# Reordering the start of a fused mLSTM and squared-ReLU FFN kernel: earlier weight words, later transposes and scores

## The chip, the cores and the metric

The kernel runs on one core of a Trainium2 chip. The time is that of one execution on the device, in microseconds. The kernel before has a median of 488.39 us in three runs (487.24 to 491.11). A profile is one further execution, recorded by the hardware profiler.

Engines are named as in the profile: PE is the matrix engine (PEld its weight loads), DVE the vector engine, ACT the scalar engine, POOL the GpSimd engine, SP the engine that issues most of the DMAs.

## The reference

There are four batches, eight heads, 768 steps and a head width of 40. For each step, an mLSTM cell updates a matrix state C and a vector n with stabilised gates, and reads them out with q:

```python
for t in range(S):
    m_new = np.maximum(f_gate[:, :, t] + m, i_gate[:, :, t])
    f_stab = np.exp(f_gate[:, :, t] + m - m_new)
    i_stab = np.exp(i_gate[:, :, t] - m_new)
    C = f_stab * C + i_stab * einsum('bhd,bhe->bhde', vt, kt)
    n = f_stab * n + i_stab * kt
    y[:, :, t] = sigmoid(o_gate[:, :, t]) * (C q) / max(|n . q|, 1)
```

The result is laid out as x with 3072 tokens of width 320. The FFN is `h = max(x @ w_in, 0)` and `out = (h * h) @ w_out`, with w_in of 320 x 2048 and w_out of 2048 x 320. The two weights come as 64-bit floats and are handed to the kernel as pairs of 32-bit words.

## The kernel before

The sequence is cut into 24 chunks of 128 steps, numbered from 0, six to a batch; chunk `s` has all eight heads. Two chunks make one of twelve groups of 256 tokens, on which the FFN works. The kernel is written in one order by hand: each engine runs its instructions in the order in which the program issues them, and waits where its operands or buffers are not ready.

For a chunk, `load_part(s, i)` loads k, q or v (i = 0, 1, 2) and `load_A(s)` loads A, the running sums of the log decay, spread over all partitions; `load_o(s)` loads the o gate. All these are DMAs on SP's queue. A is computed once for all chunks by `do_gates` on DVE, written to DRAM by `store_A`, and can be loaded from there only after that. Chunks 0 and 1 don't load A but build it on PE (`spread_mask`, `spread_A`). Then, for each chunk:

- `transposes(s)`: PE turns k and q (L553), and ACT, or DVE for chunk 1, copies them out of PSUM (L556).
- `scores(s)`: PE multiplies k and q (L587).
- `mask` (POOL, L472) and `weigh(s)` (ACT, L515 and L519) make the decay weights W; `values` (POOL, L536) scales v by W's last column for the state.
- `weighted(s)`: DVE multiplies the scores with W (L601).
- `attend(s)`: PE forms the read-out of the old state (L637), the state's increment dC (L649) and the read-out within the chunk (hp, L660). DVE adds them (L668, L831) and renews the state (L676, L678).
- `normalise(s)` makes x on DVE (L833 to L840), and `turn_rows(s)` turns x on PE (L870, L872), with a copy to xT on ACT (L875).

FFN1 of a group is done in four parts of four blocks of w_in (`ffn1(g, pp)`: L896 and L907), each followed on ACT by a relu (L920) and a square (L926). The three scratch banks `ps_at` in PSUM are used in turn by the transposes, scores, x turns and the first read-out, so a turn can wait for the copy of an older one.

The weights are brought into 32-bit floats while the attention runs, in 18 pieces: ten of w_in, numbered 0 to 9, then eight of w_out. The class `Rounding` does each piece in three steps. `fetch` loads its raw words (SP, L206). `words` splits them in two on ACT (L216, L218). `join` puts them together with three operations on DVE (L227, L231, L232) and an addition on POOL (L236), and then issues the fetch of a further piece. There are three buffers for raw words and some space lent by another tile, so a fetch waits for the join that reads its buffer. FFN1's part 0 needs pieces 0, 1 and 2, part 1 needs 3 and 4, part 2 needs 5, 6 and 7, and part 3 needs 8 and 9.

After a written-out start for chunks 0 to 2, a loop over `u` from 0 to 7 does chunks 2 to 5 in half steps, each with one FFN1 part. A second loop over `n` does the rest: parts of FFN1 and FFN2 in turn, four to a chunk, with the attention of a chunk laced in (`attend_begin`, `attend_end`). In this stretch FFN2 uses a fast product with seven multiplications for eight, which needs sums of blocks of w_out: `sums_of_weights(i)` on DVE, of which number 3 is L961, in place on w_out. `attend_begin` ends with a one-element operation on DVE (L718), for which the second half of the chunk's products on PE (L757 in `attend_end`) waits. `spread_slots(b)` issues three DMAs on POOL (L383, L385) that copy batch b's rows of A into another order in DRAM. `sums_of_x` (POOL, L1048 and L1051) makes the sums of xT for the fast FFN1.

Of the kernel before, what the change touches and what calls it, by code (L numbers as in the profile page):

```python
# [29 lines left out]
def kernel(  # L30
# [148 lines left out]
    class Rounding:  # L179
# [11 lines left out]
        def fetch(self):  # L191
            n = len(self.raws)
            if n == len(pieces):
                return
            dst, srcs = pieces[n]
            if n < LENT and n % NRAW == NRAW - 1:
                at = 2 * NPAIR * P
                raw = lent_t[:, at : at + 2 * WIDE].bitcast(I32).rearrange("p (c w) -> p c w", w=2)
            else:
                raw = conv.tile([P, WIDE, 2], I32, name="raw", bufs=NRAW - 1)  # L200
            self.raws.append(raw)
            for rows, src in srcs:
                to = raw[rows, : dst.shape[1]]
                if len(src.shape) == 4:
                    to = to.rearrange("p (a f) w -> p a f w", a=src.shape[1])
                nc.sync.dma_start(to, src)  # L206
# [200 lines left out]
    def load_o(s):  # L407
        b, c = divmod(s, NB)
        r, (s0, s1) = next((r, (a, z)) for r, (a, z) in enumerate(RUNS) if a <= s < z)
        if s == s0:  # L410
            st["og", r] = ld.tile([P, 4, H, D], F32, name="og")
        og = st.setdefault(s, {})["og"] = st["og", r][:, s - s0]
        nc.sync.dma_start(og, o_gate[b, :, c * P : (c + 1) * P, :].rearrange("h p d -> p h d"))
# [7 lines left out]
    def load_A(s):  # L421
        b, c = divmod(s, NB)
        d = st.setdefault(s, {})
        A = ld.tile([P, H, P], F32, name="A_bc", bufs=2)
        d["A"] = [A]
        if s >= ROT:
            d["A"] = [A[:].rearrange("p (x own) t -> p x (own t)", own=2)]
            for m in range(2):
                nc.sync.dma_start(
                    A[HALVES[m]].rearrange("p h t -> p (h t)"),  # L430
                    A_slots[b, c, m].rearrange("x own t -> (x own t)").unsqueeze(0).to_broadcast([DP, H * P]),
                )
            return
        nc.sync.dma_start(
            A[:].rearrange("p h t -> p (h t)"),
            A_d[c, b * H : (b + 1) * H].rearrange("h t -> (h t)").unsqueeze(0).to_broadcast([P, H * P]),
        )

    def spread_mask(s):
        H2 = H // 2  # L440
        A = ps_h.tile([P, H2, P], F32, name="A_ps", tag="h_ps")
        nc.tensor.matmul(
            A[:], lhsT=ident_h[:], rhs=later_h[:].unsqueeze(1).to_broadcast([P, H2, P]), start=True, stop=True,
            skip_group_check=True,
        )
        st.setdefault(s, {}).setdefault("A", []).append(A)
# [100 lines left out]
    def transposes(s, o=(False, False)):  # L547
        d = st[s]
        kqT(s)
        for i, n in enumerate(("kT", "qT")):  # L550
            tp = bank(o[i])
            for j in range(PR):
                nc.tensor.transpose(  # L553
                    tp[:, j, :], d["kq"][:, i, 2 * j : 2 * j + 2, :].rearrange("p h d -> p (h d)"), ident[:],
                )
            (nc.vector.tensor_copy if s == 1 else nc.scalar.copy)(d[n], tp)  # L556
# [355 lines left out]
    def ffn1(g, pp):  # L912
        ffn1_main(g, pp)
        ffn1_rest(g, pp, st["half"][0])
# [220 lines left out]
    def idle(n):  # L1135
        t = ps_h.tile([P, W], F32, name="idle", tag="h_ps")
        for _ in range(n):
            nc.tensor.matmul(
                t[:], lhsT=zeros[:, :1].to_broadcast([P, P]), rhs=zeros[:, :1].to_broadcast([P, W]), start=True, stop=True,
            )  # L1140
# [5 lines left out]
    def load_part(s, i):  # L1146
        b, c = divmod(s, NB)
        dst, src = load_parts(s)[i]
        nc.sync.dma_start(dst, src[b, :, c * P : (c + 1) * P, :].rearrange("h p d -> p h d"))
# [10 lines left out]
    load_part(1, 2)  # L1160
    load_o(0)
    load_o(1)
    idle(12)
    transposes(0)
    idle(4)
# [3 lines left out]
    rounding.words()  # L1169
    store_A()  # L1170
    load_A(2)
    load_part(2, 0)
    load_part(2, 1)
    fetch(1)
    load_part(2, 2)
    fetch(1)
    spread_A(0)
    turn_gates(i_sb, b_T)
    rounding.join()
    load_A(3)  # L1180
    load_part(3, 0)
    load_part(3, 1)
    eA_turned = turn_gates(A_sb, eA_T, later=True)
    weigh(0)
    eA_turned()
    transposes(1, (False, True))
    spread_mask(1)
    spread_mask(1)
    spread_A(1)
    scores(0)  # L1190
    weigh(1)
    scores(1, (True, True))
    rounding.words()
    first.close()
    ffn = ctx.enter_context(tc.tile_pool(name="ffn", bufs=2))
    before = ExitStack()
# [5 lines left out]
    half_tanh(0)  # L1202
    half_tanh(1)
    weighted(0)
    weighted(1)
    attend(0)
    rounding.join()
    load_part(3, 2)
    load_o(2)
    load_o(3)  # L1210
    rounding.words()
    normalise(0)
    attend(1)
    rounding.join()
    turn_rows(0)
    transposes(2)
    idle(2)
    turn_rows(1)
    rounding.words()
    scores(2)  # L1220
    weigh(2, masked=True)
    decay_old(2)
    rounding.join()


# [2 lines left out]
    for u in range(8):  # L1228
        s = 2 + u // 2
        relu_half()  # L1230
        if u % 2 == 0:
            if u == 0:
                ffn1(0, 0)
            else:
                if u == 2:
                    idle(3)
                if s - 1 < X_SQ:
                    turn_rows(s - 1)
                if u == 4:
                    square_half()  # L1240
                scores(s)
                ffn1(u // 4, u % 4)
            if u == 2:
                rounding.words()
                weigh(4, masked=True, vw=False)
                decays(4)
                rounding.words()
            weighted(s)
            if u == 0:
                mask(s + 1)  # L1250
                rounding.step()
            if u == 2:
                rounding.join()
                rounding.join()
                mask_W(4)
                values(4)
                rounding.words()
            else:
                if u == 0:
                    relu_half()  # L1260
                weigh(s + 1, masked=(u != 6), vw=(u == 6))
                if u == 4:
                    mask_W(5)
                square_half()
                if u > 0:
                    scale_q(s)
        else:
            if u == 1:
                half_tanh(2)
                half_tanh(3)  # L1270
            if u < 7:
                load_A(s + 2)
            for r in {1: (), 3: (5, 6), 5: (7,), 7: ()}[u]:
                load(r)
            if u == 5:
                for r in range(4, 8):
                    half_tanh(r)
            if s < X_SQ:
                attend(s)
            else:  # L1280
                attend_begin(s)
                attend_end(s)
                store_num(s)
            if u == 3:
                square_half()
            if u != 3:
                rounding.join(fetch=u < 7)
            if u == 1:
                load(4)
                values(s + 1)  # L1290
            if s < X_SQ:
                normalise(s)
            if u == 3:
                rounding.join()
            if u == 5:
                pair_up(7)
            if u == 7:
                load_A(7)
            if u > 4:
                load_num(s)  # L1300
            transposes(s + 1, (True, True))
            rounding.words()
            ffn1(u // 4, u % 4)
            if u != 3:
                square_half()
            if u == 5:
                decays(5)
            if u == 7:
                normalise_turned(4)
                store_rows(4)  # L1310
                rounding.fetch()
                rounding.join()
        if u < 4:
            load_o(4 + u)
        while rounding.done < NEXT[u]:
            if u == 1 and rounding.done + 1 == NEXT[u]:
                rounding.join()
            else:
                rounding.step()
        if u == 6:  # L1320
            load_squares(7)
        for x in WIN_SUMS.get(u, ()):
            sums_of_win(x)
# [21 lines left out]
    for n, (which, g, i) in enumerate(parts):  # L1345
# [52 lines left out]
        if n == 8:  # L1398
            sums(1, slice(0, NPAIR), (3,))
        if n == 9:  # L1400
            sums_of_weights(3)
            sums(1, slice(0, NPAIR), (4,))
            sums_of_weights(2)
            turn_squares(6)
# [65 lines left out]
            do(load, s + 4)  # L1470
        if n == 4:
            sums_of_weights(1)
        if n == 3:
            turn_halves()
        if n in (9, 25):
            spread_slots(2 + n // 25)
        if at == 0:
            ffn1_square()
# [33 lines left out]
```

## Time and profile before

| | |
|---|---|
| median of three runs | 488.39 us (487.24 to 491.11) |
| profiled execution | 489.48 us, with a span of 487.7 us from the first to the last instruction |
| mean granted PE clock | 0.997 of full speed |
| PE busy | 478.5 us (98% of the span) |
| DVE, ACT, POOL busy | 340.6 us, 243.1 us, 227.4 us |
| DMA | 69.92 MB, mean 143 GB/s |

By stages, DMA is near or above a full share of its sixteen engines from 10 to 70 us (0.93 to 1.17 in each 10 us) and at 0.75 to 0.78 from 140 to 300 us. ACT is busy for 9.96 of the 10 us from 40 to 50 and for 9.87 from 60 to 70.

The profile gives, for each engine, busy time and the idle time ahead of an instruction with the event that ended it. The chain of work that ended last is followed back from the last instruction, at each step to what released it. A busy PE does not say at what clock it ran; that stands in the column for the granted clock of the windows.

### The profile page before, as it was taken

How to read it: one execution, taken by the hardware profiler on the slowest of the kernel's cores; microseconds unless marked ns; L12 is line 12 of the kernel's file. 1: busy time of each engine (PE TensorE's matmuls, PEld its weight loads, DVE VectorE, ACT ScalarE, POOL GpSimd, SP SyncE). 2: the span in 40 equal slices, each digit the busy share in tenths (PEclk: the TensorE clock that was granted, in tenths of full speed). 3: DMA queues.
4: the chain of work that ended last, by engine and by line, in shares of the span. 5: the costliest groups of instructions: out<-in, count | busy, mean ns of one | idle time of the engine just before them, and what ended most of it. 6: DMA issues, size and time to landing. Idle time of an engine off the chain costs nothing.

```text
span 487.7 us, 15402 instructions
## 1 busy us (share of the span) xinstructions
PE 478.5 (98%) x6227; PEld 447.3 (92%) x6229; DVE 340.6 (70%) x719; ACT 243.1 (50%) x534; POOL 227.4 (47%) x335
## 2 busy tenths in 40 slices
PE   9999999999999999999999999998999999999997
PEld 4877887779999999999999999998999999999997
DVE  7779678887987856867866856865956956635441
ACT  4589799534742731933733931732942650513300
POOL 5454545555599087089088087088075040020000
PEclk9989999999999999999999999999999999999999
DMA  8999997779978668768768768768646613200000
GB/s 183 196 253 243 303 222 203 199 124 207 180 129 206 135 116 219 138 126 200 127 118 214 134 117 207 140 116 204 121 96 160 122 49 83 56 22 9 1 28 27
DMA packets 192695, 69.92 MB, mean 143 GB/s; under 512 B 158128, under 2 KB 181360, under 8 KB 192624
## 3 DMA queue, kind: packets, MB, share of 16 engines
q1 hardware_dynamic: 186400, 58.68, 56.9%
q0 software_dynamic: 6080, 10.16, 8.9%
q8 instruction: 49, 0.80, 0.7%
q14 instruction: 22, 0.18, 0.1%
q10 hardware_dynamic: 144, 0.10, 0.1%
HBM read 55.69 MB, written 18.92 MB: 153 GB/s over the span
## 4 chain that ended last, share of the span: by engine, by line
PE 88%; DVE 4%; DMA 3%; SPq 1%; issue 1%; POOL 1%; ACT 1%; DVEq 0%; ACTq 0%; POOLq 0%
PE h_ps L980 32%; PE h_ps L1056 25%; PE h_ps L1089 7%; PE h_ps L896 6%; PE h_ps L934 4%; PE numT L746 3%; PE numT L727 2%; PE h_ps L907 2%; PE numT L757 1%; PE h_ps L579 1%; PE tp L587 1%; DMA a_rows<-A_sb 1%; PE tp L579 1%; DMA raw<-in_moe_w_in_dram 1%; PE tp L553 1%
## 5 line engine op out<-in xcount | busy, mean ns | idle before, releaser
L478 POOL TENSOR_SCALAR_AFFINE_SELECT A_bc<-A_bc 64x512 f32<-64x512 f32 x32 | 24.9, 779 | 89.8 <-ACT kq L496 66.4
L1070 ACT COPY r_sb<-h_ps 128x512 f32<-128x512 f32 x20 | 11.7, 585 | 84.5 <-PE h_ps L1056 84.4
L980 PE MATMUL h_ps<-T,S 128*128 128x160 f32 x352 | 51.7, 300 | 0.0
L980 PE MATMUL h_ps<-w_out,g 128*128 128x160 f32 x336 | 49.4, 303 | 0.4 <-DVE w_out L961 0.4
L980 PEld LDWEIGHTS h_ps<-T,S 128*128 128x128 f32 x352 | 48.9, 190 | 0.4 <-ACT g_c L1105 0.2
L980 PEld LDWEIGHTS h_ps<-w_out,g 128*128 128x128 f32 x336 | 46.1, 190 | 2.0 <-issue 0.7
L996 DVE TENSOR_TENSOR y_sb<-y_sb,h_ps 128x160 f32<-128x160 f32 x44 | 14.0, 319 | 44.4 <-PE h_ps L980 44.2
L1056 PE MATMUL h_ps<-xT,w_in 128*128 128x128 f32 x320 | 43.3, 278 | 0.0
L1056 PE MATMUL h_ps<-lent_t,w_in 128*128 128x128 f32 x320 | 42.3, 275 | 0.0
L1056 PEld LDWEIGHTS h_ps<-xT,w_in 128*128 128x128 f32 x320 | 39.2, 192 | 1.6 <-issue 1.2
L375 POOL DMA_DIRECT2D va<-in_v_dram x64 | 39.2, 621 | 2.5 <-DMA kq_rows<-in_k_dram 1.8
L1056 PE MATMUL h_ps<-lent_t 128*128 128x128 f32 x320 | 39.1, 276 | 0.5 <-POOL lent_t L1051 0.5
L1089 PE MATMUL h_ps<-xT,w_in 64*64 64x128 f32 x960 | 39.1, 272 | 0.0
L1056 PEld LDWEIGHTS h_ps<-lent_t,w_in 128*128 128x128 f32 x320 | 38.9, 192 | 0.0
L1056 PEld LDWEIGHTS h_ps<-lent_t 128*128 128x128 f32 x320 | 37.3, 192 | 0.7 <-POOL lent_t L1051 0.7
L1089 PEld LDWEIGHTS h_ps<-xT,w_in 64*64 64x64 f32 x960 | 34.8, 133 | 1.3
L509 ACT ACTIVATE A_bc<-A_bc,b_R 128x64 f32<-128x64 f32 (+1 forms) x128 | 35.7, 361 | 0.4
L780 DVE STREAM_TRANSPOSE tn<-numT 128x256 f32<-128x256 f32 x36 | 14.1, 428 | 30.4 <-PE numT L727 21.2
L896 PE MATMUL h_ps<-xT,w_in 128*128 128x256 f32 x128 | 31.1, 398 | 0.0
L1048 POOL TENSOR_TENSOR lent_t<-xT 128x128 f32<-128x128 f32 (+1 forms) x18 | 14.6, 830 | 32.7 <-DVE xT L862 32.7
L896 PEld LDWEIGHTS h_ps<-xT,w_in 128*128 128x128 f32 x128 | 24.9, 199 | 3.9
L980 PE MATMUL h_ps<-w_out,g_c 128*128 128x160 f32 x192 | 28.0, 303 | 0.0
(223 smaller groups left out, 1148.4 us busy)
## 6 DMA issues: line engine op xcount, KB each, us to landing
A_bc<-a_slots SPq DMA_DIRECT2D x32, 256.0 KB, 4.4
kq<-num_rows SPq DMA_DIRECT2D x80, 64.0 KB, 2.5
num_rows<-tn SPq DMA_DIRECT2D x18, 256.0 KB, 2.4
raw<-in_moe_w_out_dram SPq DMA_DIRECT2D x7, 640.0 KB, 5.4
kqT<-kq_rows SPq DMA_DIRECT2D x34, 128.0 KB, 4.2
og<-in_o_gate_dram SPq DMA_DIRECT2D x24, 160.0 KB, 4.9
x_rows<-x_sb SPq DMA_DIRECT2D x20, 192.0 KB, 3.0
xT<-x_rows SPq DMA_DIRECT2D x80, 48.0 KB, 3.4
```

Source lines behind the costliest of these rows:

```text
L375: eng.dma_start(dst[HALVES[n], PR * (1 - late_keys) : PR * (2 - late_keys)], src[HALVES[late_keys], PR * m : PR * (m + 1)],)
L478: nc.gpsimd.affine_select(part, part, compare_op=ALU.is_ge, fill=-1e30, base=0, pattern=[[0, PR], [0, 2], [1, DP]], channel_multiplier=-1,)
L509: nc.scalar.activation(A[0][:, x, to], A[0][:, x, to], AF.Exp, bias=b_R[:, b, c, own, x : x + 1],)
L746: nc.tensor.matmul(d["numT"][m][HALVES[e], i, t0:], lhsT=va_w[s % NKQ][keys, at * D1 : at * D1 + DP], rhs=rhs, start=(s % NB == 0 and i == ...
L780: nc.vector.transpose(to[:, 2 * m : 2 * m + 2], d["numT"][m].rearrange("p c t -> p (c t)"))
L896: nc.tensor.matmul(hs[i][:, n, :], lhsT=w_in[:, a, fb * P : (fb + 1) * P], rhs=xT[:, :, a, :], start=(n == 0 and a == 0), stop=False,)
L934: nc.tensor.matmul(st["o_ps"][j], lhsT=st["g2", 0][:, fb, j * P : (j + 1) * P], rhs=w_out[:, fb, :], start=(fb == 0), stop=(fb == NF - 1),)
L980: nc.tensor.matmul(to, lhsT=lhsT[:, p], rhs=rhs[:, p, :], start=(start and p == 0), stop=(p == NPAIR - 1), skip_group_check=True,)
L996: add = lambda to, a, b: nc.vector.tensor_tensor(to, a, b, op=ALU.add)
L1048: sub = lambda to, a, b: eng.tensor_tensor(to, a, b, op=ALU.subtract)
L1056: nc.tensor.matmul(to[:, n, :], lhsT=lhsT[:, 4 * q + n, :], rhs=rhs, start=(start and n == 0), stop=True, skip_group_check=True,)
L1089: nc.tensor.matmul(to[cols, n, :], lhsT=w_in2[rows, 4 * q + n, cols], rhs=rhs, start=(start and n == 0), stop=True, skip_group_check=True,)
```

## The change

At the start, piece 2's fetch and the loads of k and q of chunk 2 go ahead of the load of A of chunk 2. The loads of A, k and q of chunk 3 move from before the weights of chunk 0 to after `weighted(1)`. Piece 1's words go ahead of `weigh(1)`, and its join ahead of `attend(0)`. `scores(0)` goes ahead of the masks of chunk 1. The transposes of chunk 2 go behind the second x turn, and `scores(2)` behind the first FFN1 part. Piece 3's words go behind `weigh(2)`. In the first loop, the o gates of chunks 4 to 7, one in each of the half steps 0 to 3, are loaded in two pairs in half steps 2 and 3. In the second loop, `sums_of_weights(3)` moves from part 9 to the end of part 8, and `spread_slots(2)` from part 9 to part 12.

```diff
     load_o(0)
     load_o(1)
+    fetch(1)
+    load_part(2, 0)
+    load_part(2, 1)
     idle(12)
     transposes(0)
...
     store_A()
     load_A(2)
-    load_part(2, 0)
-    load_part(2, 1)
-    fetch(1)
     load_part(2, 2)
     fetch(1)
     spread_A(0)
     turn_gates(i_sb, b_T)
     rounding.join()
-    load_A(3)
-    load_part(3, 0)
-    load_part(3, 1)
     eA_turned = turn_gates(A_sb, eA_T, later=True)
     weigh(0)
     eA_turned()
     transposes(1, (False, True))
+    scores(0)
     spread_mask(1)
     spread_mask(1)
     spread_A(1)
-    scores(0)
+    rounding.words()
     weigh(1)
     scores(1, (True, True))
-    rounding.words()
...
     weighted(0)
+    rounding.join()
+    attend(0)
     weighted(1)
-    attend(0)
+    load_A(3)
+    load_part(3, 0)
+    load_part(3, 1)
+    rounding.words()
+    normalise(0)
+    attend(1)
     rounding.join()
     load_part(3, 2)
     load_o(2)
     load_o(3)
-    rounding.words()
-    normalise(0)
-    attend(1)
-    rounding.join()
     turn_rows(0)
-    transposes(2)
     idle(2)
     turn_rows(1)
-    rounding.words()
-    scores(2)
+    transposes(2)
     weigh(2, masked=True)
     decay_old(2)
+    rounding.words()
     rounding.join()
...
             if u == 0:
                 ffn1(0, 0)
+                scores(2)
...
-        if u < 4:
-            load_o(4 + u)
+        if u in (2, 3):
+            load_o(2 * u)
+            load_o(2 * u + 1)
...
         if n == 9:
-            sums_of_weights(3)
             sums(1, slice(0, NPAIR), (4,))
...
+        if n == 8:
+            sums_of_weights(3)
...
-        if n in (9, 25):
+        if n in (12, 25):
             spread_slots(2 + n // 25)
```

## The prediction

> **What bounds the kernel now.** I read the page's busy shares first, then the chain of work that ended last, then windows of 1 us, then single engines around each idle place of PE. Times are microseconds from the span's start; "piece n" is the n-th tile of w_in words, "chunk n" the n-th block of 128 steps, both from 0; the title counts chunks from 1.
>
> ```profile
> PE 478.5 (98%) x6227; PEld 447.3 (92%) x6229; DVE 340.6 (70%) x719; ACT 243.1 (50%) x534; POOL 227.4 (47%) x335
> PE 88%; DVE 4%; DMA 3%; SPq 1%; issue 1%; POOL 1%; ACT 1%; DVEq 0%; ACTq 0%; POOLq 0%
> ```
>
> PE is busy for 478.5 of 487.7, so an order change can win at most some 9 us of waits, plus what PE loses at a low clock. The change touches two stretches: the start up to about 60, and 130 to 148. In the chain, the start reads:
>
> ```profile
> 9.18 4.81 DMA a_rows<-A_sb
> ...
> 15.99 2.79 SPq L206
> 18.83 4.47 DMA raw<-in_moe_w_in_dram
> ...
> 23.38 0.66 ACT lent_t L216
> ...
> 24.59 0.36 ACT xT L875
> ...
> 27.14 5.34 PE h_ps L896 x16
> ...
> 38.14 3.46 PE h_ps L896 x16
> ```
>
> SP waits at A of chunk 2 until the rows of A are in DRAM (13.98). Piece 2 is queued behind it and lands at 18.83 + 4.47 = 23.3. ACT has been idle for 5.8 and does piece 2's word split ahead of the x copy that frees a PSUM bank for the second x turn, so PE waits. Then the first FFN1 part takes 5.34 where the next takes 3.46. The windows say why (columns: window, busy PE, PEld, DVE, ACT, POOL, granted clock, DMA share, GB/s):
>
> ```profile
> 27.00:28.00 1.00, 1.00 (x7) 0.80 (x4) 0.77 (x2) 1.00 (x4) 0.58 (x1) 0.68 1.08 289
> 28.00:29.00 1.00, 1.00 (x4) 0.82 (x3) 0.96 (x2) 1.00 (x5) 0.00 (x0) 0.50 1.36 191
> 29.00:30.00 1.00, 1.00 (x4) 0.73 (x4) 0.24 (x2) 1.00 (x5) 0.00 (x0) 0.50 0.95 112
> 30.00:31.00 1.00, 1.00 (x4) 0.83 (x3) 1.00 (x2) 1.00 (x4) 0.85 (x2) 0.61 0.85 244
> ```
>
> The clock is halved from about 27.3 to 30.7, some 3.4 us, right after PE's one long idle (23.8 to 25.0). It is the only such drop: the mean clock is 0.997, and 0.003 x 487.7 is 1.5 us. In the second stretch the timeline shows three waits of PE and who causes them:
>
> ```profile
> 133.07 0.16 DVE L718 TENSOR_SCALAR kq<-numT 1x1 f32<-1x1 f32 x1
> 135.23 1.68 DVE L961 TENSOR_TENSOR w_out<-w_out 128x1280 f32<-128x1280 f32 x1
> 133.28 0.44 PE L757 MATMUL numT<-vw,kq 64*64 64x41 f32 x16 [0.18 <-DVE kq L718]
> 136.96 0.40 PE L980 MATMUL h_ps<-w_out,g 128*128 128x160 f32 x1 [0.39 <-DVE w_out L961]
> 143.80 1.19 POOL L385 DMA_DIRECT2D a_slots<-a_rows  x2
> 147.31 0.38 PE L1056 MATMUL h_ps<-lent_t 128*128 128x128 f32 x1 [0.50 <-POOL lent_t L1051]
> ```
>
> DVE has run without a gap from 119.5 to 133.2, so whatever is put ahead of L718 there delays PE.
>
> **What the Trainium skill says.** "TensorE: Matmul & The Clock Gate", section "Part 1: The HAM clock gate", has the array at half clock after a window of about 3.4 us with too little PE work, for windows that run freely; the trace agrees (0.50 for 3.4 us). "SBUF — State Buffer", section "Who interferes with whom", has GpSimd and a two-port VectorE instruction block each other; here L231 takes 0.43 alone and 1.38 at 31.9 beside POOL. "DMA: Bandwidth & Descriptors", section "Queues, rings and completion order", has one queue's descriptors consumed in ring order; landings follow SP's order here (A 19.1, k 20.0, q 20.6, piece 2 21.9 and 23.3), so what is issued earlier pushes the rest back.
>
> **The change part by part.**
>
> *Piece 2, k and q of chunk 2 ahead of A.* SP issues the last o gate by 13.04 and then stands 0.96 waiting for the rows of A; now piece 2 (two DMAs), k and q go out. Landing spacing in this stretch is about 2 us for 512 KB and 0.8 for 160 KB. From the last o gate at 16.4, with the gap gone, piece 2 lands at about 20 instead of 23.3, A of chunk 2 at about 22 to 23 instead of 19.1. A's mask on POOL (1.35) then ends by 24.4, before ACT wants it (26): hidden. The x copy is no longer behind late words.
>
> *Words of piece 1 ahead of the weights of chunk 1, scores of chunk 0 earlier.* ACT spends 0.67 + 0.6 on the words first, PE runs 1.06 of scores ahead of the mask: the weights end at about 16.5 instead of 15.5. Behind them on POOL are vw (0.7) and the clears of the state (0.36 each), which DVE's state copy L676 awaits: 18.2 instead of 17.5. On PE hp of chunk 0 ends near 17.8, so some 0.5 + 0.3 is waited for. DVE does piece 1's three operations (1.6) while it used to wait for scores; its chain for the two x's ends at about 23.7 (before 23.93). So x, not piece 2, is then last.
>
> *Transposes of chunk 2 behind the second x turn, scores behind FFN1.* x turn 23.75, transposes 24.4 to 25.35 with the xT copy beside them, FFN1 from 25.35 (before 27.07). With no idle of 1.2 us the clock stays up: 3.5 + 1.06 for the part, then 1.09 of scores: 31.0, where before the same work ended at 33.55. Gain 2.5, of which 1.8 is clock.
>
> *What is late next.* (a) k and q of chunk 3, now behind pieces 4 and 5, land at about 32.5 (before 30.8); PE wants them at 34.6: hidden, by 2 us. (b) Piece 4's three DVE operations now stand behind weighted(2), which waits for the scores at 31.0: from 32.3 they take 1.65 alone to 3.7 beside POOL, as before. Then POOL adds (1.27): 35.5 to 37 against PE's need at 35.7, costing 0 to 1.3. (c) The o gates of chunks 2 and 3 are behind pieces 5 and 6: the later lands at about 37 to 38.4 (before 31.36 + 3.8 = 35.2), and ACT reaches it at 37.2; behind it on ACT are the kqT copy, words of 6 and 7, a relu and the x copy, 5.3 in all, so FFN1 part 2 starts at 42.5 to 43.8, against 45.02. From there pieces land earlier (the o gates of 4 and 5 moved behind piece 13, 1.6 us of transfers), ACT's wait at 52.6 shrinks alike, and PE has no gaps. I keep 1.5 of the 2.5. Bounds: 2.5, and -0.2 if one more half-clock window (1.7) is set off by (b) or (c).
>
> *Moved loads of o gates 4 to 7.* Chunks 6 and 7 now come together; ACT uses the last at 69.5, landing about 69; up to 0.5 on ACT, whose kqT copy at 70.3 is needed at 73.3: nothing.
>
> *sums_of_weights(3) from part 9 to the end of part 8.* L961 goes ahead of L718. Alone it is about 1.48 (L954, same size, 1.48), so L718 ends near 134.7 and PE's L757 starts at 134.75 instead of 133.28: +1.5. The wait at 136.96 goes: -0.4. Bounds 0 (if DVE's run gets shorter) and +1.9. Net +1.1.
>
> *spread_slots(2) from part 9 to part 12.* Three POOL issues (0.61 + 1.19) no longer stand ahead of vw and the sums of x: the wait at 147.31 goes, -0.5 (or 0, if the delay of +1.1 already covers it). At part 12 they lie before a mask that follows 10 us of POOL issues; the same sum as before.
>
> Sum: -1.5 + 1.1 - 0.5 = -0.9. The profiled execution took 489.48 (span 487.70 plus 1.78 around it), 1.09 above the median of 488.39; so 488.6 against that one, and 487.5 as a median.
>
> **The rivals.** *All of it kept:* DVE and POOL collide less, PE holds its 2.5, L961 finds a gap: -2.5 - 0.4 - 0.5 = -3.4, 485.0. For it: ACT waits 2.25 at 33.5 and 2.1 at 52.6 for raw words that now come earlier. Against: ACT is 99% busy from 40 to 50, DVE 85%. *The clock stays:* PE's new small waits still leave a slow window; FFN1 starts 1.7 earlier but runs at half clock, and 1.2 survives: -0.7 + 1.1 - 0.5, 488.3. *Slower: chunk 3's mask on POOL.* It stands ahead of piece 4's add, and A of chunk 3 is now behind pieces 4 and 5. If A lands at T, the add ends at T + 2.6, PE wants it at 35.7. At my T of 31.5 it is harmless; from T = 33.1 PE waits, and a wait over 1 us brings back a half-clock window. At T = 34.8 that is 1.7 + 1.7, so the start gives -2.5 + 3.4 = +0.9, and with +0.6 from parts 8 to 11 about 489.9. It decides from T about 34.
>
> **How the numbers follow.** Chances: forecast 0.40, all kept 0.15, clock stays 0.20, slower by the mask 0.25. 487.5 is the likeliest. The low end takes in the first rival, 485.0; the high end the last one and some of T being later still, 490.8. One per cent is 4.9 us, about what a measurement of this kernel can tell from no change (the three runs spread over 3.9). Faster by more needs all of PE's early waits and more: 0.03. Slower by more needs several slow windows, 0.10 out of the last rival. Within: 0.87.
>
> **What would show it.** Right: piece 2 landing near 20, FFN1's first part near 3.5 with the clock at 1.0 from 26 to 32, the second x turn waiting for DVE's x; L757 waiting over 1 us for L718 behind L961; no wait for lent_t L1051. Wrong: a clock of 0.5 anywhere in 20 to 60; PE waiting for POOL w_in in FFN1 part 1; ACT waiting for the o gate for over 2 us.

## The result

The changed kernel takes a median of 493.57 us (491.97 to 497.55, 11 runs), the kernel before 488.39 us (486.65 to 491.11, 11 runs). The ratio is 1.0109, with a 95% interval of 1.0078 to 1.0140: slower by about 5.2 us, where 0.9 us faster was forecast. A second measurement beside the experiments gave 1.0090 (1.0059 to 1.0121). The profiled execution of the kernel after took 497.13 us with a span of 495.4, against 489.48 and 487.7 before.

The page's busy shares and the shares of the chain, kernel after:

```profile
PE 483.7 (98%) x6229; PEld 450.7 (91%) x6229; DVE 340.6 (69%) x719; ACT 243.5 (49%) x534; POOL 224.7 (45%) x335
...
PE 82%; DMA 5%; ACT 4%; DVE 4%; SPq 2%; issue 2%; POOL 0%; DVEq 0%
```

PE does the same work and is busy 5.2 us longer: it ran longer at a low clock. The mean clock of this execution is 0.986, against 0.997. The windows of 1 us show where (columns: window, busy PE, PEld, DVE, ACT, POOL, granted clock, DMA share, GB/s):

```profile
17.00:18.00 1.00, 1.00 (x9) 0.89 (x8) 0.35 (x2) 0.25 (x1) 1.00 (x4) 1.00 1.12 259
18.00:19.00 1.00, 0.56 (x4) 0.58 (x3) 0.97 (x3) 0.47 (x1) 1.00 (x1) 0.70 1.47 165
19.00:20.00 1.00, 1.00 (x7) 1.00 (x6) 0.93 (x5) 0.00 (x0) 0.85 (x2) 0.50 1.12 99
...
27.00:28.00 1.00, 1.00 (x6) 0.47 (x6) 0.93 (x3) 0.11 (x1) 0.00 (x0) 0.50 0.92 370
28.00:29.00 1.00, 1.00 (x8) 0.67 (x9) 0.36 (x1) 0.35 (x1) 0.49 (x1) 0.68 1.18 325
29.00:30.00 1.00, 1.00 (x10) 0.95 (x8) 0.00 (x0) 0.87 (x3) 0.78 (x1) 1.00 1.29 183
...
141.00:142.00 1.00, 1.00 (x26) 0.82 (x16) 0.53 (x2) 0.00 (x0) 0.62 (x1) 0.64 0.75 117
142.00:143.00 1.00, 1.00 (x5) 1.00 (x5) 1.00 (x4) 0.00 (x0) 0.32 (x1) 0.50 0.35 69
```

The clock is halved from about 18.4 to 28.6, three stretches of 3.4 us on end, and once more from 141.3 to 144.7. Below, such a stretch is called a drop; it costs half its length, 1.7 us, and takes 0.0035 off the mean clock of a 488-us execution, so (1 - mean clock) / 0.0035 counts drops in each run. In the profiles it gives 4 for this kernel (0.986) and 1 for the kernel before (0.997), as many as their windows show. The eleven runs of the kernel after have 2.7 on average and none is without. Each group of drops follows a wait of PE that is new. The first, in the timelines of POOL, DVE and PE (start, duration, what, and in brackets the idle time ahead with what ended it):

```profile
16.53 0.74 POOL L536 TENSOR_TENSOR vw<-va,g_c 128x328 f32<-128x328 f32 x1 [2.10 <-ACT dec L519]
17.21 0.72 POOL L1197 MEMSET Co<- 128x352 f32 x2
...
17.63 0.67 DVE L676 COPY Co<-dC 64x164 f32<-64x164 f32 x2 [1.74 <-POOL Co L1197]
...
18.45 1.97 PE L637 MATMUL hi<-Co,kqT 128*128 128x82 f32 x8 [0.44 <-DVE Co L676]
...
27.34 0.63 PE L870 MATMUL tp<-ident,x_sb 128*128 128x128 f32 x2
...
29.50 3.62 PE L896 MATMUL h_ps<-xT,w_in 128*128 128x256 f32 x16
```

Piece 1's words stand ahead of chunk 1's weights on ACT, so vw comes late on POOL, the zeroing of the state late behind it, DVE's copy after that, and PE waits 0.44 us. Everything up to FFN1 then runs at half speed (hi 1.97 where it takes 1.10 at full clock), and FFN1 starts at 29.50, not at 27.07 as before, although PE no longer waits ahead of the second x turn (27.34), which has nothing in brackets. The second wait, DVE and PE:

```profile
138.78 1.48 DVE L961 TENSOR_TENSOR w_out<-w_out 128x1280 f32<-128x1280 f32 x1
140.29 0.16 DVE L718 TENSOR_SCALAR kq<-numT 1x1 f32<-1x1 f32 x1
...
140.50 0.44 PE L757 MATMUL numT<-vw,kq 64*64 64x41 f32 x16 [1.60 <-DVE kq L718]
```

Of the 7.7 us by which the profiled span grew, three more drops are 5.1 us and the wait at L757 is 1.4 us more. The remaining 1.2 us are more than covered by two further new waits. An o gate of chunks 6 and 7 comes late for ACT, and PE waits for ACT's work behind it: 0.98 us at 77.72 (ACT's copy of kqT ends at 77.68; the profile names an operation of DVE that ends with it) and 0.94 us at 81.81. The profile before has neither. ACT, and then PE:

```profile
74.88 0.47 ACT L417 ACTIVATE og<-og 128x320 f32<-128x320 f32 x1 [2.33 <-DMA og<-in_o_gate_dram]
...
81.81 1.99 PE L896 MATMUL h_ps<-xT,w_in 128*128 128x256 f32 x8 [0.94 <-ACT g L920]
```

### The profile page after: what moved, and what is told of

It is laid out like the page before. It is cut to its first block, busy times and chain, and to the rows that moved or that the text cites. A ratio compares the mean times of both kernels' runs of the same rounds, so it can differ in the third digit from the quotient of the medians.

```text
span 495.4 us, 15405 instructions
## 1 busy us (share of the span) xinstructions
PE 483.7 (98%) x6229; PEld 450.7 (91%) x6229; DVE 340.6 (69%) x719; ACT 243.5 (49%) x534; POOL 224.7 (45%) x335
## 4 chain that ended last, share of the span: by engine, by line
PE 82%; DMA 5%; ACT 4%; DVE 4%; SPq 2%; issue 2%; POOL 0%; DVEq 0%
PE h_ps L980 34%; PE h_ps L1056 24%; PE h_ps L1089 7%; PE h_ps L934 4%; PE numT L746 3%; DMA og<-in_o_gate_dram 2%; PE numT L727 2%; DMA A_bc<-a_rows 2%; ACT g_c L515 1%; PE numT L757 1%; PE h_ps L579 1%; PE h_ps L896 1%; DMA kqT<-kq_rows 1%; PE tp L579 1%; DMA kq<-in_k_dram 1%
## 5 line engine op out<-in xcount | busy, mean ns | idle before, releaser
L478 POOL TENSOR_SCALAR_AFFINE_SELECT A_bc<-A_bc 64x512 f32<-64x512 f32 x32 | 23.6, 738 | 88.8 <-ACT kq L496 75.5
L980 PE MATMUL h_ps<-w_out,g 128*128 128x160 f32 x336 | 50.8, 309 | 0.0
L980 PEld LDWEIGHTS h_ps<-w_out,g 128*128 128x128 f32 x336 | 47.7, 195 | 1.3 <-issue 0.7
L1056 PEld LDWEIGHTS h_ps<-xT,w_in 128*128 128x128 f32 x320 | 39.2, 192 | 1.7 <-issue 1.2
L1056 PEld LDWEIGHTS h_ps<-lent_t 128*128 128x128 f32 x320 | 37.3, 192 | 0.0
L896 PE MATMUL h_ps<-xT,w_in 128*128 128x256 f32 x128 | 30.1, 384 | 1.4 <-ACT g L920 0.9
L896 PEld LDWEIGHTS h_ps<-xT,w_in 128*128 128x128 f32 x128 | 23.4, 190 | 5.7 <-ACT g L920 1.3
```

Source lines behind the costliest of these rows:

```text
L478: nc.gpsimd.affine_select(part, part, compare_op=ALU.is_ge, fill=-1e30, base=0, pattern=[[0, PR], [0, 2], [1, DP]], channel_multiplier=-1,)
L896: nc.tensor.matmul(hs[i][:, n, :], lhsT=w_in[:, a, fb * P : (fb + 1) * P], rhs=xT[:, :, a, :], start=(n == 0 and a == 0), stop=False,)
L980: nc.tensor.matmul(to, lhsT=lhsT[:, p], rhs=rhs[:, p, :], start=(start and p == 0), stop=(p == NPAIR - 1), skip_group_check=True,)
L1056: nc.tensor.matmul(to[:, n, :], lhsT=lhsT[:, 4 * q + n, :], rhs=rhs, start=(start and n == 0), stop=True, skip_group_check=True,)
```

## The experiments

All ratios are to the kernel before, run beside them; its executions there have about one drop on average (0.9 to 1.0), and 28 to 39% of them none. A drop costs this kernel some 1.4 us: of its executions beside the first four experiments, those without a drop have a median of 489.13 us (18), those with one 490.10 (22), those with two 491.89 (13). An idle product, made by `idle(n)`, multiplies zeros and its result is not read. `after_again` is the whole change once more.

| kernel | ratio (95% interval) | drops, mean | runs without a drop |
|---|---|---|---|
| after_again | 1.0090 (1.0059 to 1.0121) | 2.6 | 0 of 11 |
| start_only | 1.0074 (1.0045 to 1.0103) | 2.5 | 0 of 12 |
| sums_only | 1.0032 (1.0014 to 1.0049) | 1.2 | 5 of 22 |
| slots_only | 1.0006 (0.9987 to 1.0025) | 0.9 | 10 of 22 |
| after_idle9 | 1.0058 (1.0027 to 1.0088) | 2.4 | 0 of 10 |
| start_memset_dve | 1.0007 (0.9987 to 1.0027) | 0.4 | 12 of 14 |
| start_fill | 1.0017 (0.9997 to 1.0038) | 0.1 | 21 of 22 |
| start_words_back | 1.0118 (1.0085 to 1.0151) | 3.2 | 0 of 6 |
| start_fill_og_early | 0.9995 (0.9973 to 1.0017) | 0.2 | 20 of 22 |
| after_both_fills | 1.0014 (0.9995 to 1.0034) | 0.1 | 20 of 22 |
| sums_fill | 1.0002 (0.9981 to 1.0023) | 1.0 | 7 of 22 |
| before_zero_four | 1.0008 (0.9988 to 1.0028) | 2.6 | 0 of 21 |
| before_zero_six | 1.0053 (1.0032 to 1.0073) | 3.0 | 0 of 22 |
| before_idle7 | 0.9985 (0.9968 to 1.0001) | 0.2 | 19 of 22 |
| before_idle7_slots | 0.9973 (0.9951 to 0.9995) | 0.1 | 20 of 22 |

### Which part costs

The change was cut in three: the start alone (with the o gates), the move of `sums_of_weights(3)` alone, the move of `spread_slots(2)` alone. A fourth kernel is the whole change with PE's wait at L757 filled with six idle products.

```diff
 # start_only, against after
-        if n == 8:
-            sums_of_weights(3)
         if n == 9:
+            sums_of_weights(3)
-        if n in (12, 25):
+        if n in (9, 25):
 # after_idle9, against after
+            if n == 9:
+                idle(6)
             do(attend_end, s)
```

`sums_only` and `slots_only` are the same lines the other way round, put into the kernel before.

> The changed kernel with its two late moves taken back (sums_of_weights(3) and spread_slots(2) at part 9 again). Theory A, the late move of sums_of_weights(3) is a large part of the loss: the 1.6 us wait for L718 and the half-clock window after it (3.4 us at half speed, so 1.7 us) go, the old 0.4 us wait comes back: 490.5 to 491.0. Theory B, the loss is made at the start alone: 493.5 as with the whole change.

> The kernel before with only sums_of_weights(3) moved to the end of part 8. Theory A: L757 waits some 1.5 us for L718, a half-clock window follows, the 0.4 us wait for L961 goes: +2.3 to +2.9 us, so 490.7 to 491.3. Theory B: the move is covered, 488.4.

> The kernel before with only spread_slots(2) moved to part 12. The prediction: the 0.5 us wait of PE for lent_t (L1051) goes, 487.9. The rival: POOL is late with vw for another reason (it waits for ACT), so the wait stays and nothing changes: 488.4.

> The changed kernel with six idle matmuls put on PE at part 9, where it waits 1.6 us for L718; the wait itself is as long. If the half clock from 141.4 to 144.8 comes from this wait, it goes and with it 1.7 us: 491.9. If the clock drops for another reason, or the idle matmuls don't count as work, 493.5 or a little more.

Measured: 1.0074, 1.0032, 1.0006 and 1.0058. The first three add up to 1.0112, the whole to 1.0109 and 1.0090, so the parts are close to additive, and two thirds of the loss lies in the start. `start_only` has its drops there too (windows):

```profile
18.00:19.00 1.00, 0.58 (x5) 0.61 (x6) 0.97 (x3) 0.00 (x0) 1.00 (x1) 1.00 1.42 158
...
21.00:22.00 1.00, 1.00 (x7) 1.00 (x7) 0.74 (x2) 0.07 (x1) 0.00 (x0) 0.52 0.97 269
...
27.00:28.00 1.00, 1.00 (x7) 1.00 (x6) 0.00 (x0) 0.46 (x1) 0.64 (x1) 0.56 1.05 348
```

The drop begins 2.5 us after the wait here and at once in the kernel after: the wait is the same, its place against the drop's start isn't. In both it lies within the 3.4 us ahead of the drop (about 17.6 to 21.0 here, 15.0 to 18.4 there). `sums_only` shows the forecast wait at L757, and its profiled execution has a clock of 1.000, so this wait alone does not always bring a drop (PE timeline):

```profile
135.10 0.44 PE L757 MATMUL numT<-vw,kq 64*64 64x41 f32 x16 [1.60 <-DVE kq L718]
```

In `after_idle9` PE has no wait at L757 in that half step, and no drop from 136 to 150; the drops of the start are left. On average it has 2.4 drops against 2.6 in `after_again`, so this wait brings few of them.

### Is it the wait for Co, and how

`start_memset_dve` takes away what makes Co late, `start_fill` leaves it late and gives PE two idle products meanwhile, `start_words_back` puts piece 1's words back. All start from `start_only`.

```diff
 # start_memset_dve
-        nc.gpsimd.memset(x[:], 0.0)
+        nc.vector.memset(x[:], 0.0)
 # start_fill, in attend(s), ahead of the old-state products
             if s == 1:
                 mask(2)
+                idle(2)
 # start_words_back
-    rounding.words()
     weigh(1)
     scores(1, (True, True))
+    rounding.words()
```

> start_only with the two state tiles zeroed on DVE instead of POOL. Theory (the wait of the old-state products for Co, then half-clock windows): in start_only Co's zeroing sat on POOL at 17.2 behind vw of chunk 1 at 16.5, DVE's state copy waited 1.96 us for it, and TensorE waited 0.45 us. DVE is idle from 15.6 to 17.6, so the copy now follows dC at about 16, the 0.45 us wait goes, and with it the windows from 21 to 27.6: mean clock up from about 0.991 to 0.996, time down by 2 to 3.5 us from start_only, ratio to the kernel before 0.999 to 1.003. Rival (the windows come from something else in the start, such as the shorter run of matmuls ahead of it): the wait goes but the clock stays, ratio 1.006 to 1.008.

> start_only with two idle products of 0.43 us put before the old-state products of chunk 1, to fill TensorE's wait for Co. Theory (an unfilled wait of 0.45 us brings the windows): Co's copy ends at the same 18.3, the two idle products cover the wait and reach about 0.4 us past it; windows before 28 us gone, ratio 1.000 to 1.004. Rival (the wait isn't what brings them): clock as in start_only, ratio 1.008 to 1.009.

> start_only with the words of piece 1 back behind the weights and scores of chunk 1. Theory (those ACT and DVE operations made dec, vw and Co of chunk 1 late): Co's copy back at about 16.9, no wait of TensorE at 18.4, clock in the start back to one window or none; time 2 us below start_only, ratio 1.001 to 1.005 (piece 1 is late instead, some 0.5 to 1 us at the first or second FFN1 part). Rival (the words' place doesn't matter): ratio 1.007.

`start_memset_dve`: the copy on DVE starts at 16.45, PE does not wait, FFN1 starts at 24.69, and the ratio falls from 1.0074 to 1.0007. `start_fill`, PE timeline:

```profile
17.75 0.60 PE L1139 MATMUL idle<-zeros 128*128 128x512 bf16 x2
18.36 1.09 PE L638 MATMUL hi<-Co,kqT 128*128 128x82 f32 x8
...
23.61 0.41 PE L871 MATMUL tp<-ident,x_sb 128*128 128x128 f32 x2 [0.21 <-DVE x_sb L841]
...
25.25 3.62 PE L897 MATMUL h_ps<-xT,w_in 128*128 128x256 f32 x16
```

The old-state products start at 18.36, as late as in `start_only` (18.42): the wait is as long, it is only no longer idle. Yet 21 of 22 executions have no drop, where `start_only` had 2.5 on average, and the ratio is 1.0017. So the idle, not the delay, brings the drops. The idle products also add dense work, but `start_memset_dve` adds none, and in its profile that place has no drop either. It has one later, from 34 to 38, after another wait amid small products (0.88 us at 32.20). FFN1 of `start_fill` starts at 25.25; the prediction had 25.35.

`start_words_back` came out the other way from what was expected, 1.0118. Its DVE and PE show why:

```profile
17.04 1.10 DVE L227 TENSOR_SCALAR mag<-mag 128x512 f32<-128x512 f32 x1 [3.23 <-ACT mag L216]
...
19.25 0.66 DVE L676 COPY Co<-dC 64x164 f32<-64x164 f32 x2
...
20.05 1.70 PE L637 MATMUL hi<-Co,kqT 128*128 128x82 f32 x8 [2.11 <-DVE Co L676]
```

Piece 1's join stayed ahead of `attend(0)` on DVE. With the words late on ACT, DVE waits in front of the join and Co's copy stands behind it. So in this order words and join belong together, and the longer wait (2.11 us) came with more drops (3.2).

### The wait alone, in the order of before

Here the first state tile is zeroed four or six times on POOL, and nothing is moved.

```diff
     for x in C_flat:
-        nc.gpsimd.memset(x[:], 0.0)
+        for _ in range(4 if x is C_flat[0] else 1):
+            nc.gpsimd.memset(x[:], 0.0)
```

> The kernel before, in its own order, with the first of the two state tiles zeroed four times on POOL instead of once (1.08 us more on POOL at 16.4), so that Co is late and nothing else is moved. DVE's copy then ends at about 18.6 and TensorE, which reaches the old-state products at 17.94, waits 0.6 to 0.7 us. Theory (that wait alone brings the half-clock windows, whatever the order around it): mean clock 0.990 to 0.993, two to three windows instead of 0.9, time up by 2.5 to 4 us, ratio 1.005 to 1.009. Rival (it needs the change's other moves too): one window as before, ratio 1.001 to 1.002 for the wait.

> As before_zero_four with six times, so a wait of about 1.3 us. Theory: ratio 1.007 to 1.012, no fewer windows than before_zero_four. Rival: ratio 1.003 for the wait, one window as before.

The wait of 0.90 us (0.6 to 0.7 was expected) does bring the drops, 2.6 on average and in every execution; the reorder is not needed for them. But the price that was expected for them did not come: 1.0008 with four, 1.0053 with six. The PE timeline of `before_zero_four`:

```profile
18.88 1.97 PE L637 MATMUL hi<-Co,kqT 128*128 128x82 f32 x8 [0.90 <-DVE Co L676]
20.65 3.55 PE L660 MATMUL tp<-va,g_c 128*128 128x41 f32 x16
...
29.25 0.38 PE L870 MATMUL tp<-ident,x_sb 128*128 128x128 f32 x2
```

The second x turn (29.25) no longer waits. Before, PE waits there 1.23 us in its profile, and 1.7 and 2.7 us in those of `sums_only` and `slots_only`, whose start is the same. It waits for ACT's copy of the first x turn, which stands behind the words of piece 2 (the copy ends at 24.96, PE starts at 25.01; the second x is ready at 23.93). A slow PE fills that wait, and the kernel before pays for about one drop anyway. So, as an estimate, 2.6 drops (4.4 us) less 1.0 (1.8 us), with the new wait of 0.9 us and without one of 1.2 to 2.7 us, leave 0.8 to 2.3 us; measured are 0.4 us for four (0.0008 x 491, interval -0.6 to 1.4). For six, with 3.0 drops and a wait of 1.79 us, it is 2.4 to 3.9 us, and 2.6 us are measured (1.6 to 3.6). Both lie at the low end.

The reordered start has hardly any such wait left (0.2 us), so drops there cost most of their price: with two (3.4 us) FFN1 starts at 28.02 in `start_only`, with three (5.1 us) at 29.50 in the kernel after, with none at 25.25 in `start_fill`, so 2.8 and 4.2 us later.

### Both waits filled, and what is left

```diff
 # after_both_fills, against after: idle(2) as in start_fill, idle(6) as in after_idle9
 # sums_fill: sums_only with that idle(6)
 # start_fill_og_early, against start_fill
-        if u in (2, 3):
-            load_o(2 * u)
-            load_o(2 * u + 1)
+        if u in (1, 2):
+            load_o(2 * u + 2)
+            load_o(2 * u + 3)
```

> The whole change once more, for a figure beside the other three. Ratio to the kernel before 1.008 to 1.012, mean clock 0.986 to 0.993.

> The whole change, with two idle products ahead of the old-state products of chunk 1 and six ahead of the end of the attention in half step 9 of the later part, 0.25 us each at full clock, so that both of TensorE's new waits (0.45 us for Co, 1.6 us for the scaled q) are filled. No wait gets shorter by it. Theory (most of the loss is half-clock windows that follow these two waits): mean clock 0.998 to 1.0, ratio 1.001 to 1.004, of which 1.2 us is the wait of 1.6 us itself. Rival (the loss is in the transfers and engines behind, and the clock only accompanies it): ratio 1.007 or more.

> The kernel before with only the sums of the weights of chunk 3 moved, and six idle products in the wait of 1.6 us. Theory (the wait costs its 1.2 us more than before, and a half-clock window only in some executions): ratio 1.002 to 1.003, against 1.0032 unfilled. Rival (the windows carried most of that loss): ratio 1.000 to 1.001.

> start_fill with the output gates of chunks 4 to 7 asked for one turn earlier: the pairs at the second and third of the eight parts of FFN1, not at the third and fourth. In start_fill ACT waited 0.46 and 0.52 us for the gates of chunks 6 and 7, which came at 68.2 and 69.7, and TensorE waited 0.5 us for its relu at 75.8 and ran 4.25 of 5 us busy between 75 and 80. Theory (the pair that is asked for late takes the 0.9 us back that the start had gained by 53 us): those waits go, FFN1 at 81.0 instead of 81.7, ratio 0.7 to 1 us below start_fill: 0.999 to 1.001. Rival (the gates only filled a wait that ACT has anyway): ratio as start_fill, 1.0017; or, if the earlier gates push chunk 3's v or A back on the queue, more.

`after_both_fills` is the whole change with eight idle products of about 0.25 us added: 1.0014 instead of 1.0090. That difference, 0.0076 or 3.7 us, is the share of the loss that the two unfilled waits carry through the clock (2.5 drops fewer are 4.2 us). `sums_fill` came to 1.0002, nearer to the rival's figure, though its drops (1.0) fell by only 0.2 from `sums_only`; the two intervals overlap, so how the 1.6 us of `sums_only` divide between wait and drop stays open.

In `start_fill` too ACT waits for the o gates and PE for ACT, by less than in the kernel after (timelines):

```profile
68.22 0.47 ACT L417 ACTIVATE og<-og 128x320 f32<-128x320 f32 x1 [0.46 <-DMA og<-in_o_gate_dram]
...
69.72 0.47 ACT L417 ACTIVATE og<-og 128x320 f32<-128x320 f32 x1 [0.52 <-DMA og<-in_o_gate_dram]
...
75.80 1.99 PE L897 MATMUL h_ps<-xT,w_in 128*128 128x256 f32 x8 [0.48 <-ACT g L921]
```

With the gates asked for earlier these waits go and others come: in `start_fill_og_early`

```profile
56.21 1.99 PE L897 MATMUL h_ps<-xT,w_in 128*128 128x256 f32 x8 [1.02 <-ACT g L921]
...
62.83 2.45 ACT L515 ACTIVATE g_c<-A_bc,b_T 128x128 f32<-128x128 f32 x8 [0.60 <-DMA A_bc<-a_rows]
```

and the last FFN1 part of this stretch starts at 83.04, where it starts at 81.70 in `start_fill`, 82.25 in `before_idle7` (old places of the gates, where ACT waits 1.37 us for one) and 81.89 in the profile before. In these profiles, whichever load goes first on SP's queue, another is late. By time the two new placements can't be told apart (1.0017 and 0.9995, with overlapping intervals); the old places of the gates with the new start were not run.

### A version that beats both

The kernel before can have its own drop filled: seven idle products instead of two ahead of the second x turn. The second kernel adds the one part of the change that cost nothing, `spread_slots(2)` at part 12.

```diff
-    idle(2)
+    idle(7)
     turn_rows(1)
...
-        if n in (9, 25):
+        if n in (12, 25):
             spread_slots(2 + n // 25)
```

> The kernel before with seven instead of two idle products ahead of the second turn of rows, so that TensorE's wait of 1.2 to 2.7 us at 24 to 26 is filled. Theory (the half-clock window at 27 to 31 is brought by that wait): clock in the start 1.0, 1.0 to 1.7 us gained in those executions that had a window, none lost in the others, as x is not ready earlier; ratio 0.996 to 0.999. Rival (the idle products run on past the end of the wait or don't keep the clock): ratio 1.000 to 1.002.

> The kernel before with seven idle products ahead of the second turn of rows and only the move of spread_slots(2) from the change: the two edits that cost nothing on their own (ratios 0.9985 and 1.0006). Expected 0.997 to 1.000: the windows of the start gone, the wait of 0.5 us at 147 gone or hidden. Rival (the slots collide with the masks of part 12): 1.000 to 1.002.

`before_idle7` is at 0.9985, its interval reaching 1.0001; `before_idle7_slots` at 0.9973 (0.9951 to 0.9995), some 1.3 us faster than before and, by the two ratios, nearly 6 us faster than the change (1.0090). PE timeline of `before_idle7`:

```profile
23.08 1.69 PE L1138 MATMUL idle<-zeros 128*128 128x512 bf16 x7
...
25.41 0.44 PE L870 MATMUL tp<-ident,x_sb 128*128 128x128 f32 x2 [0.65 <-ACT xT L875]
...
27.48 3.72 PE L896 MATMUL h_ps<-xT,w_in 128*128 128x256 f32 x16
```

The idle is cut to 0.65 us, and 19 of 22 executions have no drop; FFN1 begins no earlier than before (27.07) but takes 3.72 instead of 5.41. That the slots' move adds to it is not shown: the two intervals overlap widely.

## Why the prediction was wrong

*What bounds, and the first drop.* Right in reading (one drop, after PE's idle at 24), wrong in the lesson drawn. I tied a drop to an idle of over 1 us. A wait of 0.45 us amid the small products of the attention brings 2.5 on average. The Trainium skill, "TensorE: Matmul & The Clock Gate", section "Why this matters for your kernels", warns of gaps over some 3 us; here 0.44 us was enough (the kernel after), and the measurement decides.

*Piece 2, k and q of chunk 2.* Right: ACT takes piece 2 up at 20.55 as it lands; 20 was forecast.

*Words of piece 1 ahead of the weights of chunk 1.* The chain was right down to the wait: vw, the zeroing, L676, PE short of work for half a microsecond. I priced the wait and not what follows it. In this stretch of small products the wait had two prices: its length, which later waits may hide, and the clock.

*Transposes and scores: the step that failed.* "With no idle of 1.2 us the clock stays up" was the mistake, made in the paragraph after the one in which the new wait of half a microsecond had been found. With that idle filled the step's own numbers hold: FFN1 at 25.25 (25.35 forecast), part 2 at 43.41 (42.5 to 43.8 forecast). With it empty, the start has 2.5 drops where the kernel before has 1 and the forecast none. By the count they are worth up to 2.5 x 1.7 = 4.3 us; measured, filling this one wait takes the start from 1.0074 to 1.0017, so 2.8 of the 6.1 us between forecast (-0.9) and result (+5.2).

*What is late next, and o gates 4 to 7 at nothing.* "I keep 1.5 of the 2.5" failed as well, and by nearly as much: at full clock `start_fill` comes out at +0.8 us (interval -0.1 to 1.9), not at -1.5. The gain was there at first. With no drop in either, the scores behind FFN1 part 0 are done, and the next products (hi) begin, at 30.76 in `start_fill` and at 32.19 in `before_idle7`, which has the old order. By part 2 it is nearly gone, because PE waits in both for the same addition on POOL, that of piece 6:

```profile
43.13 1.33 POOL L236 TENSOR_TENSOR w_in<-mag,low 128x512 int32<-128x512 int32 x1 [2.81 <-DVE mag L232]
44.51 3.29 PE L897 MATMUL h_ps<-xT,w_in 128*128 128x256 f32 x14 [0.40 <-POOL w_in L236]
...
43.28 1.32 POOL L236 TENSOR_TENSOR w_in<-mag,low 128x512 int32<-128x512 int32 x1 [2.54 <-DVE mag L232]
44.65 3.29 PE L896 MATMUL h_ps<-xT,w_in 128*128 128x256 f32 x14 [0.21 <-POOL w_in L236]
```

(The first two lines are `start_fill`, the others `before_idle7`.) The fourth part starts at 53.30 and 53.44; it starts at 54.24 in the profile before, which has a drop. So the new order's own lead there is 0.14 us: what remained of the forecast gain was clock, and the fill of the old order has that too. Among the executions without a drop `start_fill` is even slower than `before_idle7`, at a median of 490.83 us (21) against 489.63 (19); the 1.2 us between them are 0.4 to 2.9 by resampling (95%). The moved o gates, forecast to cost nothing, don't explain it: PE's waits behind late ones are 1.9 us in the profile of the kernel after and 0.5 us in `start_fill`, but 0.9 us in `before_idle7` too, with the old places. What does is not settled: the profiles of `start_fill` and before are level at 133 us (133.60 against 133.79 at L727), and the stretch from L757 to the end takes 352.2 to 355.2 us from profile to profile where no drop falls in it.

*sums_of_weights(3).* The wait was right: L961 ahead of L718, 1.60 us (1.5 forecast), the wait for L961 gone. +1.1 was forecast, 1.6 us measured (0.7 to 2.4); in the profile of the kernel after a drop follows, which I had not priced. With the wait filled 1.0002 is left, so whether its length cost the forecast 1.1 us stays open.

*spread_slots(2).* -0.5 was forecast, +0.3 us measured with an interval of -0.6 to 1.2: nothing that can be told. The four terms' misses (2.8 and 2.3 us in the start, 0.5 and 0.8 us in the two late moves) add up to 6.4 us, about the 6.1 us to be explained.

*The rivals.* "The clock stays" named the cause, but at one drop instead of several, at 488.3. In "Slower by chunk 3's mask on POOL" the wait came, but not behind the mask and at a small price. In the kernel after PE's weight load for FFN1 part 1 waits for piece 4's addition, and the part takes 3.98 us instead of 3.62. POOL had ended the mask at 38.05 and was idle until DVE handed over piece 4. (DVE's L231 takes 1.20 us beside the mask, 0.43 alone, so the mask may have a part in that.) POOL and PEld:

```profile
36.77 1.28 POOL L472 TENSOR_SCALAR_AFFINE_SELECT A_bc<-A_bc 128x1024 f32<-128x1024 f32 x1
39.20 1.27 POOL L236 TENSOR_TENSOR w_in<-mag,low 128x512 int32<-128x512 int32 x1 [1.16 <-DVE mag L232]
...
40.53 2.89 PEld L896 LDWEIGHTS h_ps<-xT,w_in 128*128 128x128 f32 x14 [0.50 <-POOL w_in L236]
```

That is the forecast's point (b), priced at 0 to 1.3 us (its own times, 32.3 + 1.65 or 3.7 + 1.27, end at 35.2 to 37.3, not at 35.5 to 37). All three of my signs for a wrong forecast are in the profile of the kernel after: a clock of 0.5 between 20 and 60, PE waiting for POOL's w_in in part 1, and ACT waiting over 2 us for an o gate.

## What to carry to other kernels

Before an order change is priced, look for each new wait of PE in a stretch of small products, and price it twice: its own length, and the half-clock stretches that may follow. If it can't be removed, two idle products in it may be worth more than several reordered steps: 0.5 us of empty work took back 2.8 us here. A stretch with slack behind it (a wait of 1.2 us or more at the second x turn) hides part of the drops, of which a tightened one pays most, so a tighter order needs its waits filled first. And follow a gain to the next thing that PE waits for: 1.4 us won by 31 us were gone at 44.5 us, where both orders wait for the same weights.

## What the runs showed of the hardware that was not expected

- With an idle of 0.45 us every execution of `start_only` lost clock worth two to four half-clock stretches of 3.4 us (mean clock 0.985 to 0.993); the same delay filled with two 128x512 products left one execution of 22 with a drop. Products of 128x41 and 128x82 kept PE at full clock in the kernel before (1.00 in each microsecond from 18 to 24) and did not bring it back in the kernel after, where PE is busy and the clock stays at 0.50 from 19 to 28.
- Not each wait does it: 0.89 us at 76 us and 0.64 us at 137 us (in `before_idle7`) were followed by none in an execution with a mean clock of 1.0, and 1.60 us at 135 us by none in `sums_only`. These three have dense FFN products at once or within a microsecond behind them. But the same two executions also have 0.65 us at 25.4 and 1.68 us at 25.6 with no drop behind, and there FFN1 follows two microseconds later. What decides is not settled: neither the density of the work nor the place of the wait was varied alone.
